# Packed attention and a gelu feed-forward layer on one core: the product of packed queries and w_in remade in float32 tiles, with a new order

## The chip, the cores and the metric

One core of a Trainium2 chip runs the whole program. The metric is the device time of one execution in microseconds; the median of three runs stands for a kernel. Engines: TensorE (matmuls), VectorE, ScalarE, GpSimd, and SP, which issues all transfers. In rows of the profile they are PE (PEld for its weight loads), DVE, ACT, POOL and SP.

## What is computed

```python
def _attn_ref(q, k, v, p):          # q, k, v: (8, 8, 576, 64), p: (8, 8, 32, 64)
    scale = 1.0 / np.sqrt(q.shape[-1])
    def sm_attn(qq, kk, vv):
        s = scale * np.matmul(qq, kk.transpose(0, 1, 3, 2))
        s = s - np.max(s, axis=-1, keepdims=True)
        a = np.exp(s)
        a = a / (np.sum(a, axis=-1, keepdims=True) + 1e-09)
        return np.matmul(a, vv)
    p_packed = sm_attn(p, k, v)
    return sm_attn(q, p_packed, p_packed)
def _moe_ref(x, w_in, w_out):       # x: (4608, 512), the heads side by side
    h = x @ w_in                    # w_in (512, 2048), w_out (2048, 512), both 64-bit floats
    g = 0.5 * h * (1.0 + erf(h / np.sqrt(2.0)))
    return g @ w_out
```

## The kernel before, in words

The packed queries (32 for each of 8 heads) are computed first. As x is attention weights times packed queries, x @ w_in is taken as attention weights times (packed queries times w_in). That inner product, `wps`, replaces a large one: for each batch it has 8 x 32 = 256 rows.

The eight batches go in four pairs, the hidden layer in four blocks of 512 columns (FB). A pair and a block make a **unit** u, 16 in all, with eight **steps** n each: two batches j times four chunks c of 128 hidden columns. A step is one group of the first product `h` (L1050: wp times a2T, twelve matmuls of 288 columns; in unit 0 plain float32, L1041), a gelu on ScalarE (L1077), a split of the result into a high and a low half (g: L1083 on ScalarE, L1084 on VectorE), and twelve matmuls of the second product `o` (L1104 to L1106) with w_out. Rows left over by 576 = 4.5 x 128 go into `o_edge` at a unit's end. Numbers that enter a matmul are split into halves of type float32r and multiplied in three matmuls, high by high, high by low, low by high; the low half is number minus high half. Plain float32 matmuls appear in the profile as two records each.

The product that is changed is `packed_w_in` (L950). For a pair of batches `ph` holds the packed queries in block form, 128 columns for each of four slots (a slot is two heads, 128 rows of w_in), with zeros elsewhere, split into halves by GpSimd (`packed_split`, L661). With w_in's halves it takes three matmuls a slot (L968 to L970), in two groups of two slots. A group's result is copied from PSUM in pieces of 64 partitions: four casts on ScalarE (L986), four subtractions on VectorE (L990). In unit 0 the product is plain float32 (L964), in halves of 256 columns, one batch at a time.

The weights arrive as 64-bit floats and are decoded to float32 on the chip (`decode`, L886): two ScalarE instructions (L906, L907), three on VectorE (L916, L917, L922), and GpSimd adds (L938, L928) and takes low halves (L884). In units 0 to 3 every slot i of a unit (0 to 3 of w_in, 4 to 7 of w_out) is decoded and its halves stored to scratch memory (`keep`); units 4 to 15 reload them. In unit 0, w_in is decoded in halves of 256 columns and its float32 form is used before the split.

Attention of pair 0 runs at the start, chunk by chunk (a chunk is four heads of a batch): packed scores `s` (L483, eight matmuls on tiles of 64x32), exponentials, `pp` (L623), a transpose, ppT, the second scores, maxima, centring, exponentials, weights a2. Pairs 1 to 3 run it beside the units of the pair before. While it has nothing to do at the start, TensorE multiplies `still`, an idle product (L1023).

The order of the work is set by a planner inside the kernel (class `Order`). Each piece of work (`Op`) has an engine, a cost and a step number; an engine that is free in the plan takes the ready piece of lowest step number. Buffers are rings: a piece that needs one waits until it is given back. The tables FIRST (unit 0 and pair 0), LATER (the other pairs) and LEAD (weights, `wps`) hold the step numbers. The plan fixes the order of instructions on each engine and of transfers on SP's queue, and semaphores do the waiting on the chip.

Of the kernel before, what the change touches and what calls it, by code (L numbers as in the profile page):

```python
# [10 lines left out]
F32 = mybir.dt.float32  # L11
# [55 lines left out]
LEAD = {"load": 4.4, "decode": -3.6, "packed_w_in": 4}  # L67

FIRST = {
    "p": (-200.0, -193.0),  # L70
    "k": (-186.0, -199.0, -185.0, -182.0),
    "v": (-195.0, -197.0, -181.0, -179.0),
    "q": (-183.0, -191.0, -178.0, -177.0),
    "w": (-187.0, -198.0, -194.0, -188.0, -192.0, -184.0, -190.0, -196.0, -189.0, -180.0, -176.0, -175.0),
    "scores1": (-29.0, -55.27, -22.89, -50.0),
    "softmax1": (-53.13, -50.0, -30.0, -29.0),
    "packed": (-48.76, -31.48, -27.58, -51.55),
    "scores2": (-51.65, -51.18, -34.07, -27.2),
    "softmax2": (-49.06, -48.66, -3.32, 1.29),
    "weights2": (-4.59, -15.04, -24.74, -16.37),  # L80
    "decode": (-45.0, -37.0, -20.64, -35.16, -36.53, -35.0, -50.97, -46.0, 1.0, 8.37, -33.0, 2.0),
    "packed_w_in": (-7.62, -48.76, -38.15, -25.99),
    "packed_split": (8.53, 1.15, 2.3, -11.78),
    "weights_split": (7.2, 1.11, -2.81, -0.07),
    "w_in_split": (-17.7, 3.0, 5.95, 3.0),
    "groups1": ((0,), (1,), (2,), (3,)),
    "groups2": ((0,), (1,), (2,), (3,)),
    "gpsimd": (0, 1, 2, 3),
    "copy": ("DVE", "ACT", "DVE", "ACT", "ACT", "ACT", "DVE", "DVE"),
    "low": (0, 3, 4, 5),  # L90
    "banks": (False, False, False, False),
    "turn": {"k": ("ACT", "DVE", "ACT", "ACT"), "q": ("DVE", "DVE", "ACT", "ACT")},
# [42 lines left out]
class Op:  # L135
# [3 lines left out]
    def __init__(self, engine, cost, step, fn, takes=(), table=None, busy=True):  # L139
        self.engine, self.cost, self.step, self.fn = engine, cost, step, fn  # L140
        self.takes, self.table, self.busy = takes, table, busy


class Order:
# [71 lines left out]
    def issue(self, engine):  # L216
# [50 lines left out]
def packed_attention_gelu_ffn(ctx: ExitStack, tc: tile.TileContext, q, k, v, p, w_in, w_out, out):  # L267
# [59 lines left out]
    wis.names = [f"w_{u}_{i}" for u in range(NU) for i in range(4)]  # L327
    wos.names = [f"w_{u}_{i}" for u in range(NU) for i in range(4, 8)]
# [22 lines left out]
    ph = [const.tile([P, 2, 4 * P], F32R, name=f"ph{i}") for i in range(2)]  # L351
    for t in ph:
        nc.gpsimd.memset(t.bitcast(F32), 0.0)

    plain_ph = accs.take("ph")
    nc.gpsimd.memset(plain_ph, 0.0)


    pp_ready = {(b, hh): Event() for b in range(B) for hh in range(2)}
    plain_ready = {(b, hh): Event() for b in range(2) for hh in range(2)}  # L360
# [5 lines left out]
    a2T, plain_a2 = {}, {}  # L366
# [110 lines left out]
    def products(ts, lhs, rhs, swap=0):  # L477

        for n in range(2):
            rows = slice(64 * n, 64 * n + 64)  # L480
            for g in range(4):
                r0 = 32 * (g ^ 2 * swap)
                nc.tensor.matmul(  # L483
                    ts[n][r0:r0 + 32, :HALF], lhsT=lhs[n][rows, 32 * g:32 * g + 32], rhs=rhs(g)[rows],
                    start=True, stop=True)

    def scores_of_batch(bt, name, which, lhs, evacuate, engine, cost, step):
        xTs = [bt.xT[name, c].rearrange("p (g x) -> p g x", g=2) for c in range(2)]

        def part(half):  # L490
# [4 lines left out]
                    (t[:, 0], t[:, 1]), lhs, lambda g: xTs[g // 2][:, g % 2, cols], which == 2 and bt.j),  # L495
# [82 lines left out]
    def packed(s, step):  # L578
# [659 lines left out]
```

## Time and profile before

| | |
|---|---|
| median of 3 runs | 769.54 us (769.28 to 769.65) |
| profiled execution | 768.53 us, its span 766.7 us |
| TensorE busy | 743.2 us, 97% of the span |
| VectorE busy | 458.5 us, 60% |
| ScalarE busy | 413.7 us, 54% |
| GpSimd busy | 204.7 us, 27% |
| moved by transfers | 123.5 MB |

The span is the time between the first and the last instruction of the profiled execution; that execution's own time holds 1.8 us around it. Busy is the union of an engine's instructions. TensorE's matmuls are pipelined and the ends in the records are modelled, so the distance from one start to the next says what a matmul costs, and an average of 97% says nothing about the stretches in which it waits.

### The profile page before, as it was taken

What the parts mean: (1) busy time and instruction counts of PE and PEld (TensorE: products, weight loads), DVE (VectorE), ACT (ScalarE), POOL (GpSimd) and SP (SyncE); (2) the same over time, 40 slices, a digit from 0 to 9 for tenths busy, and PEclk for the clock granted to TensorE, in tenths of its full rate; (3) what the DMA queues carried; (4) which work ended last, traced back from release to release, by engine and by line L of the source; (5) the groups of instructions that cost most, each with busy time, mean ns of one, the idle gap of its engine ahead of it and who ended that gap; (6) DMA issues with size and microseconds to landing.
All of it is one profiled execution on the core that took longest, in us unless ns stands there. A gap on an engine that the chain in (4) does not pass through costs nothing.

```text
span 766.7 us, 12964 instructions
## 1 busy us (share of the span) xinstructions
PE 743.2 (97%) x4948; PEld 621.5 (81%) x4948; DVE 458.5 (60%) x733; ACT 413.7 (54%) x714; POOL 204.7 (27%) x401
## 2 busy tenths in 40 slices
PE   9889998898999999999999999999999999999998
PEld 7667776676778888888778888888878888888886
DVE  5999767988787543446478643356479522352522
ACT  4888866859667254437447345336546354333421
POOL 3568535764541111111122111111122111111110
PEclk9999999999999999999999999999999999999999
DMA  9859995656744899334443799324542523222021
GB/s 301 301 205 208 219 275 187 232 183 172 273 142 164 206 160 223 127 125 100 144 142 141 183 193 214 148 103 94 170 144 110 190 98 116 103 97 72 6 105 69
DMA packets 159293, 123.53 MB, mean 161 GB/s; under 512 B 124416, under 2 KB 132608, under 8 KB 159232
## 3 DMA queue, kind: packets, MB, share of 16 engines
q1 hardware_dynamic: 159232, 122.71, 56.7%
q8 instruction: 39, 0.64, 0.4%
q14 instruction: 22, 0.18, 0.1%
HBM read 96.47 MB, written 26.21 MB: 160 GB/s over the span
## 4 chain that ended last, share of the span: by engine, by line
PE 77%; DVE 7%; DMA 6%; ACT 5%; SPq 2%; issue 1%; POOL 1%; ACTq 0%; POOLq 0%; DVEq 0%
PE h L1050 22%; PE o L1104 14%; PE o L1106 13%; PE o L1105 13%; DMA wraw<-in_moe_w_in_dram 2%; DMA wraw<-in_moe_w_out_dram 2%; DMA v<-in_v_dram 2%; PE o_edge L1104 2%; PE o_edge L1106 2%; PE o_edge L1105 2%; PE s L483 2%; PE wps L968 2%; PE wps L969 2%; PE wps L970 2%; ACT graw L1077 1%
## 5 line engine op out<-in xcount | busy, mean ns | idle before, releaser
L1077 ACT ACTIVATE graw<-h 128x576 f32<-128x576 f32 x128 | 102.4, 802 | 227.9 <-PE h L1050 173.4
L1050 PEld LDWEIGHTS h<-a2T,wp 128*128 128x128 f32 x1440 | 203.0, 189 | 15.1 <-DVE wp L990 2.6
L1050 PE MATMUL h<-a2T,wp 128*128 128x288 f32 x1440 | 211.6, 296 | 3.3 <-DVE wp L990 2.0
L1104 PE MATMUL o<-w,g 128*128 128x512 f32 x508 | 203.8, 401 | 0.9 <-ACT g L1083 0.9
L1106 PE MATMUL o<-w,g 128*128 128x512 f32 x508 | 199.8, 393 | 2.8 <-DVE g L1084 2.7
L1105 PE MATMUL o<-w,g 128*128 128x512 f32 x508 | 199.0, 392 | 0.0
L1084 DVE TENSOR_TENSOR g<-graw,g 128x512 fp32r<-128x512 f32 x128 | 96.5, 754 | 159.6 <-ACT g L1083 154.9
L1094 POOL CAST t<-graw 128x64 fp32r<-128x64 f32 x128 | 42.0, 328 | 434.9 <-ACT graw L1077 429.4
L1106 PEld LDWEIGHTS o<-w,g 128*128 128x128 f32 x508 | 95.9, 189 | 26.0 <-DVE g L1084 4.9
L1104 PEld LDWEIGHTS o<-w,g 128*128 128x128 f32 x508 | 96.1, 189 | 24.7 <-issue 6.0
L990 DVE TENSOR_TENSOR wp<-wps,wp 64x512 fp32r<-64x512 f32 x120 | 79.9, 687 | 50.1 <-ACT wp L986 48.7
L1105 PEld LDWEIGHTS o<-w,g 128*128 128x128 f32 x508 | 96.1, 189 | 16.5
L1165 DVE TENSOR_TENSOR acc<-o,acc 128x512 f32<-128x512 f32 x96 | 63.9, 685 | 35.8 <-PE o L1106 35.8
L1083 ACT CAST g<-graw 128x512 fp32r<-128x512 f32 x128 | 79.6, 623 | 2.6
L986 ACT CAST wp<-wps 64x512 fp32r<-64x512 f32 x120 | 66.7, 581 | 17.5 <-PE wps L970 16.4
L938 POOL TENSOR_TENSOR wt<-wt 128x512 int32<-128x512 int32 x28 | 38.0, 1359 | 39.9 <-DVE wt L922 39.9
L1095 POOL TENSOR_TENSOR t<-graw,t 128x64 fp32r<-128x64 f32 x128 | 45.8, 358 | 10.2
L906 ACT ACTIVATE wt<-wraw 128x512 f32<-128x512 f32 (+1 forms) x36 | 22.5, 626 | 28.5 <-DMA wraw<-in_moe_w_in_dram 15.7
L884 POOL TENSOR_TENSOR w<-wt,w 128x512 fp32r<-128x512 f32 x26 | 36.4, 1398 | 1.9 <-POOL wt L938 0.5
L412 DVE STREAM_TRANSPOSE kT<-k 128x1152 f32<-128x1152 f32 x12 | 16.5, 1376 | 21.5 <-DMA k<-in_k_dram 21.4
L922 DVE SCALAR_TENSOR_TENSOR wt<-wraw,wt 128x512 int32<-128x512 int32 (+1 forms) x36 | 26.6, 740 | 0.8
L1023 PE MATMUL idle<-still 128*128 128x256 bf16 x168 | 25.4, 294 | 1.5 <-DVE still L347 1.1
(139 smaller groups left out, 808.3 us busy)
## 6 DMA issues: line engine op xcount, KB each, us to landing
w<-ws SPq DMA_DIRECT2D x96, 512.0 KB, 5.0
ws<-w SPq DMA_DIRECT2D x32, 512.0 KB, 4.4
out_dram<-acc SPq DMA_DIRECT2D x36, 256.0 KB, 2.1
v<-in_v_dram SPq DMA_DIRECT2D x16, 512.0 KB, 5.2
wraw<-in_moe_w_out_dram SPq DMA_DIRECT2D x16, 512.0 KB, 5.0
k<-in_k_dram SPq DMA_DIRECT2D x48, 144.0 KB, 4.6
q<-in_q_dram SPq DMA_DIRECT2D x48, 144.0 KB, 5.1
wraw<-in_moe_w_in_dram SPq DMA_DIRECT2D x12, 512.0 KB, 4.3
```

What stands on the lines that cost most here:

```text
L986: (nc.vector.tensor_copy if engine == DVE else nc.scalar.copy)(hi.bitcast(F32) if plain(u) else hi, x)
L990: nc.vector.tensor_tensor(lo, x, hi.bitcast(F32), ALU.subtract)
L1050: nc.tensor.matmul(t[:, half, :HALF], lhsT=w[:, wpart, ch, fc], rhs=a2T[b, ch][:, apart, half * HALF:(half + 1) * HALF], start=ch == 0 and ...
L1077: lambda raw: nc.scalar.activation(*dst_src(raw), AF.Gelu), [(graws, f"graw_{n}")], table="gelu")
L1083: g = yield Op(ACT, 0.52, lead, lambda g: nc.scalar.copy(g[:, 0], main), [(gts, f"g_{n}")])
L1084: yield Op(DVE, 0.6, lead, lambda: nc.vector.tensor_tensor(g[:, 1], main, g[:, 0].bitcast(F32), ALU.subtract))
L1094: nc.gpsimd.tensor_copy(dst[:, 0], side)
L1095: nc.gpsimd.tensor_tensor(dst[:, 1], side, dst[:, 0].bitcast(F32), ALU.subtract)
L1104: nc.tensor.matmul(t, lhsT=g[0], rhs=w[:, 0], start=first, stop=False)
L1105: nc.tensor.matmul(t, lhsT=g[0], rhs=w[:, 1], start=False, stop=False)
L1106: nc.tensor.matmul(t, lhsT=g[1], rhs=w[:, 0], start=False, stop=last)
L1165: yield Op(DVE, 0.6, n, lambda: nc.vector.tensor_tensor(a, x, a, ALU.add))
```

## The change

A slot of w_in is now 128 rows in another arrangement: 64 dims of head g in the partitions 0 to 63, of head g + 4 in 64 to 127, two values of g side by side. So there are two w_in slots of double width for a unit (i is 0 or 1; w_out has 2 to 5), each loaded in two pieces of 256 columns, and each piece by two transfers of 64 partitions. w_in stays plain float32: one buffer a slot, no split; what is stored and reloaded is half as much. `pp` holds the packed queries of a batch without zeros, and the product is `products`, the function of the scores: eight float32 matmuls on 64x32 tiles, for one batch at a time. The result comes from PSUM in one cast and one subtraction over 128 partitions x 1024. `ph` and its split are gone. The planner keeps marked pieces of VectorE (port) and all pieces of GpSimd from overlapping in the plan. The tables are new. Rings: `wi` three buffers instead of four, `wp1` one instead of two, `sm` six instead of four, `pn` two instead of one.

```diff
 LATER = {
-    "p": (-29.7, 4.9),
+    "p": (-43.8, -18.8),
...
-LEAD = {"load": 4.4, "decode": -3.6, "packed_w_in": 4}
+LEAD = {"load": 4.9, "decode": -5.3, "packed_w_in": 2.9}
...
+            if op.port:
+                begin = max(begin, self.port)
             end = begin + op.cost
+            if op.port:
+                self.port = end
...
-    wis = ring("wi", 4, [P, 2, FB], F32R)
+    wis = ring("wi", 3, [P, 2, FB])
...
-    wps = [ring("wp0", 1, [P, 2, 2, FB], F32R), ring("wp1", 2, [P, 2, 2, FB], F32R)]
+    wps = [ring(f"wp{j}", 1, [P, 2, 2, FB], F32R) for j in range(2)]
+    pps = ring("pp", 4, [P, P])
...
-    def products(ts, lhs, rhs, swap=0):
+    def products(ts, lhs, rhs, size=HALF):
         for n in range(2):
             rows = slice(64 * n, 64 * n + 64)
             for g in range(4):
-                r0 = 32 * (g ^ 2 * swap)
+                cols = slice(32 * g, 32 * g + 32)
                 nc.tensor.matmul(
-                    ts[n][r0:r0 + 32, :HALF], lhsT=lhs[n][rows, 32 * g:32 * g + 32], rhs=rhs(g)[rows],
-                    start=True, stop=True)
+                    ts[n][cols, :size], lhsT=lhs[n][rows, cols], rhs=rhs(g)[rows], start=True, stop=True)
...
-        s.ppT = yield Op(ACT, 0.16, step + 2, lambda t: nc.scalar.copy(t, bank(m)[:, :P]), [(ppts, f"ppT_{s.n}")])
+        both = pp[s.b] = yield from one(pps, f"pp_{s.b}", ACT, step + 2)
+        rows = slice(64 * s.hh, 64 * s.hh + 64)
+        yield Op(ACT, 0.16, step + 2, lambda: nc.scalar.copy(both[rows], bank(m)[rows, :P]))
+        fire(pp_ready[s.b])
+        if s.b < 2:
+            s.ppT = yield Op(
+                DVE, 0.19, step + 2, lambda t: nc.vector.tensor_copy(t, bank(m)[:, :P]), [(ppts, f"ppT_{s.n}")])
...
+            src = w_in.rearrange("(hh g d) n -> hh d g n", hh=2, g=4)
+            c0 = f * FB + part * (FB // 2)
+            for hh in range(2):
+                nc.sync.dma_start(
+                    t[64 * hh:64 * hh + 64].rearrange("p (g n) -> p g n", g=2),
+                    src[hh, :, 2 * i:2 * i + 2, c0:c0 + FB // 2].bitcast(I32))
...
         def product(t):
-            for e in range(2):
-                slot = 2 * hh + e
-                cut = slice(slot * P, slot * P + P)
...
-                base, w = ph[pr % 2][:, :, cut], wi[u, 2 * hh + e][:, :, cols]
-                nc.tensor.matmul(t[:, e, :m], lhsT=base[:, 0], rhs=w[:, 0], start=True, stop=False)
-                nc.tensor.matmul(t[:, e, :m], lhsT=base[:, 0], rhs=w[:, 1], start=False, stop=False)
-                nc.tensor.matmul(t[:, e, :m], lhsT=base[:, 1], rhs=w[:, 0], start=False, stop=True)
+            products((t[:, 0], t[:, 1]), [pp[b]] * 2, lambda g: wi[u, g // 2][:, g % 2, cols], m)
...
-        yield Op(engine, (0.32 + 0.75 * m / FB) * n, step, high)
-        for e in range(0 if plain(u) else 2):
-            yield Op(DVE, (0.07 + 0.58 * m / FB) * n, step, lambda: low(halves[n * e:n * e + n]))
+        yield Op(engine, 0.12 + 0.87 * m / FB, step, high)
+        if not plain(u):
+            yield Op(DVE, 1.2, step, lambda: nc.vector.tensor_tensor(lo, x, hi.bitcast(F32), ALU.subtract))
...
-            start(all_packed_w_in(u, (0, 1), [8 * u - LEAD["packed_w_in"]]))
+            for j in range(2):
+                start(packed_w_in(u, j, 0, 8 * u + 4 * j - LEAD["packed_w_in"]))
```

How the order moves instructions is shown at three places. The lines in these rows are those of the kernel they come from. First, TensorE around its first group of `h`, before:

```order
L1023 MATMUL idle<-still 128x256
L964 MATMUL wps_1_1_1_912<-w_2_285,ph 128x256
L964 MATMUL wps_1_1_1_912<-w_3_222,ph 128x256
L1041 MATMUL h_918<-a_0_642,wp_0_92 128x288 x4
L1023 LDWEIGHTS still
```

And with the change (L981 is `h`, L481 `products`, L620 `pp`, L1046 to L1048 are `o`; an output called idle is a PSUM buffer that the idle product named first):

```order
L620 MATMUL idle<-v_1_750,e1T_1_755 32x64 x20
L981 MATMUL h_839<-a_0_552,wp_0_84 128x288 x4
L634 MATMUL ppTm_1_849<-ident,pn_1_845 128x128
L481 MATMUL s_1_0_852<-qT_0_612,ppT_0_835 32x288 x8
...
L981 MATMUL h_877<-a_0_552,wp_0_84 128x288 x4
L481 MATMUL wps_1_1_893<-w_0_78,pp_792 32x256 x2
L481 MATMUL wps_1_1_893<-w_1_79,pp_792 32x256 x2
...
L1046 MATMUL idle<-w_2_430,g_873 128x512
```

All eight half products and all score groups of pair 0 stood ahead of the first `h`; now the two of batch 1 and two of its score groups stand behind it, and two `h` instead of three stand ahead of the first `o`.

Second, VectorE at the product of unit 1, before (the operands named wp_0 and wp_1 are the two batches):

```order
L1084 TENSOR_TENSOR g_1266<-graw_1250,g_1266 128x512
L990 TENSOR_TENSOR wp_0_1071<-wps_0_0_0_1252,wp_0_1071 64x512
L990 TENSOR_TENSOR wp_1_1244<-wps_0_0_0_1252,wp_1_1244 64x512
...
L990 TENSOR_TENSOR wp_0_1071<-wps_1_0_0_1268,wp_0_1071 64x512
L990 TENSOR_TENSOR wp_1_1244<-wps_1_0_0_1268,wp_1_1244 64x512
...
L916 TENSOR_SCALAR wt_5_0_1347<-wt_5_0_1347 128x512
```

With the change:

```order
L940 TENSOR_TENSOR wp_0_1031<-wps_0_0_1182,wp_0_1031 128x1024
L873 TENSOR_SCALAR wt_3_0_1207<-wt_3_0_1207 128x512
L874 TENSOR_SCALAR wt_3_0_1207<-wt_3_0_1207 128x512
...
L1025 TENSOR_TENSOR g_1253<-graw_1238,g_1253 128x512
L410 STREAM_TRANSPOSE kT_1_1304<-k_1_1174 128x1152
L1025 TENSOR_TENSOR g_1289<-graw_1285,g_1289 128x512
L940 TENSOR_TENSOR wp_1_1231<-wps_1_0_1276,wp_1_1231 128x1024
```

Eight subtractions in a row became two, one for each batch, with eight instructions between them.

Third, TensorE in unit 4, at the product for unit 5, before:

```order
L970 MATMUL wps_0_0_0_3199<-w_1_2812,ph_79 128x512
L1104 MATMUL o_0_3212<-w_4_2526,g_3158 128x512
...
L1106 MATMUL o_3_3231<-w_4_2526,g_3158 128x512
L1050 MATMUL h_3239<-a2T_0_2907,wp_1_2702 128x288 x6
L1050 MATMUL h_3239<-a2T_1_2944,wp_1_2702 128x288 x6
...
L968 MATMUL wps_1_0_0_3276<-w_2_2871,ph_79 128x512
```

With the change:

```order
L481 MATMUL wps_0_0_3138<-w_0_2586,pp_2022 32x512 x2
L481 MATMUL wps_0_0_3138<-w_1_2976,pp_2022 32x512 x2
...
L990 MATMUL h_3147<-a2T_0_2644,wp_1_2763 128x288 x6
L990 MATMUL h_3147<-a2T_1_2796,wp_1_2763 128x288 x6
L1046 MATMUL o_0_3075<-w_4_2884,g_3124 128x512
...
L1048 MATMUL o_3_3094<-w_4_2884,g_3124 128x512
L990 MATMUL h_3187<-a2T_0_2601,wp_0_2989 128x288 x6
```

The product of batch 0 (wp_0) stands one `h` and one step of `o` ahead of the `h` that uses it; that of batch 1 follows four steps later.

## Rows read from the trace of the kernel before

**Rows 1.** Stretches: length; PE, PEld, DVE, ACT, POOL busy (instructions); clock; DMA share; GB/s.
```profile
0.00:64.40 64.40, 58.04 (x614) 43.23 (x614) 53.41 (x113) 44.25 (x93) 33.92 (x49) 1.00 0.79 262
64.40:225.00 160.60, 147.58 (x965) 117.80 (x966) 131.03 (x187) 120.11 (x197) 93.31 (x118) 0.98 0.77 217
...
225.00:762.70 537.70, 537.14 (x3370) 460.47 (x3369) 273.32 (x434) 249.38 (x425) 77.50 (x235) 1.00 0.49 133
```
**Rows 2.** TensorE's waits, 65.6 to 225 us: total, times, longest.
```profile
PE e1Tm L585 <- ACT graw L1077: 3.6, 2, 2.3
PE o L1106 <- DVE g L1084: 2.7, 3, 1.1
PE h L1050 <- DVE wp L990: 2.0, 1, 2.0
```
**Rows 3.** Timeline of TensorE near 706 us: start, duration, instruction.
```profile
705.99 0.40 PE L968 MATMUL wps<-w,ph 128*128 128x512 f32 x1
...
707.39 0.39 PE L1104 MATMUL o<-w,g 128*128 128x512 f32 x1
```
**Rows 4.** The same, near 347 us: one group of scores.
```profile
347.00 0.40 PE L1106 MATMUL o<-w,g 128*128 128x512 f32 x1
347.33 0.72 PE L483 MATMUL s<-kT,pT 64*32 64x288 f32 x16
347.98 0.50 PE L1104 MATMUL o<-w,g 128*128 128x512 f32 x1
348.31 0.39 PE L1105 MATMUL o<-w,g 128*128 128x512 f32 x1
348.55 0.39 PE L1106 MATMUL o<-w,g 128*128 128x512 f32 x1
```
**Rows 5.** The same, near 291 us: two groups of scores.
```profile
291.03 0.39 PE L1106 MATMUL o<-w,g 128*128 128x512 f32 x1
...
292.48 0.50 PE L1104 MATMUL o<-w,g 128*128 128x512 f32 x1
292.82 0.40 PE L1105 MATMUL o<-w,g 128*128 128x512 f32 x1
```
**Rows 6.** Instruction groups from 225 us on: busy, mean ns, idle before.
```profile
L986 ACT CAST wp<-wps 64x512 fp32r<-64x512 f32 x96 | 53.5, 581 | 16.9 <-PE wps L970 15.8
...
L990 DVE TENSOR_TENSOR wp<-wps,wp 64x512 fp32r<-64x512 f32 x96 | 64.0, 687 | 46.6 <-ACT wp L986 45.4
```
**Rows 7.** VectorE's instruction groups up to 64.4 us.
```profile
L917 DVE TENSOR_SCALAR wt<-wt 128x256 int32<-128x256 int32 x8 | 4.7, 589 | 0.3
L646 DVE COPY ph<-ppT 64x64 f32<-64x64 f32 x8 | 4.5, 569 | 0.1
...
L917 DVE TENSOR_SCALAR wt<-wt 128x512 int32<-128x512 int32 x5 | 3.8, 758 | 0.2
...
L986 DVE COPY wp<-wps 64x256 f32<-64x256 f32 x6 | 2.5, 422 | 0.1
...
L427 DVE COPY qT<-qm 128x384 f32<-128x384 f32 x4 | 2.0, 545 | 0.0
L884 DVE TENSOR_TENSOR w<-wt,w 128x512 fp32r<-128x512 f32 x2 | 1.5, 771 | 0.3 <-ACT w L935 0.3
```
**Rows 8.** Timeline of VectorE, then of GpSimd, near 60 us.
```profile
59.60 1.21 DVE L916 TENSOR_SCALAR wt<-wt 128x512 f32<-128x512 f32 x1
...
59.24 1.29 POOL L884 TENSOR_TENSOR w<-wt,w 128x512 fp32r<-128x512 f32 x1
```
**Rows 9.** Transfers: issues, KB each, median us from issue to landing.
```profile
w<-ws SPq DMA_DIRECT2D x96, 512.0 KB, 5.0
...
v<-in_v_dram SPq DMA_DIRECT2D x16, 512.0 KB, 5.2
...
v<-in_v_dram SPq DMA_DIRECT2D x16, 64.0 KB, 5.0
```
**Rows 10.** Timeline of TensorE at its first group of `h`.
```profile
57.00 2.16 PE L1041 MATMUL h<-a,wp 128*128 128x288 f32 x8
```

More of the change, by code (lines that the diff above doesn't have):

```diff
@@ L135, with __init__ @@
 class Op:
-    def __init__(self, engine, cost, step, fn, takes=(), table=None, busy=True):
+    def __init__(self, engine, cost, step, fn, takes=(), table=None, busy=True, port=False):
         self.engine, self.cost, self.step, self.fn = engine, cost, step, fn
         self.takes, self.table, self.busy = takes, table, busy
+        self.port = (engine == POOL and cost > 0) or port
 class Order:
@@ L348, in packed_attention_gelu_ffn @@
     make_identity(nc, ident)
[L351 to L360, printed above, removed]
+    pp_ready = [Event(2) for _ in range(B)]
     a2_ready = [Event(2) for _ in range(B)]
@@ L675, in scores2_of_chunk @@
         ts = yield Op(
-            PE, 0.68, step, lambda *ts: products(banks(*ts), [s.ppT] * 2, lambda g: xT[:, g], s.bt.j), takes, busy=False)
+            PE, 0.68, step, lambda *ts: products(banks(*ts), [s.ppT] * 2, lambda g: xT[:, g]), takes, busy=False)
         ts = ts if len(takes) > 1 else [ts]
         xts.give(s.bt.xT["q", s.hh])
-        start(free_ppT(s))
+        ppts.give(s.ppT)
         def turned():
@@ L745, in weights2 @@
         yield Op(DVE, 1.1, step, inverse)
-        yield Op(engine, cost, step, lambda: on(engine).tensor_tensor(u, u, per_block(r), ALU.mult))
+        yield Op(engine, cost, step, lambda: on(engine).tensor_tensor(u, u, per_block(r), ALU.mult), port=True)
         if s.b < 2:
@@ L759, in weights2 @@
         yield Op(
-            engine, cost, step, lambda: on(engine).tensor_tensor(t[:, 1], raw, t[:, 0].bitcast(F32), ALU.subtract))
+            engine, cost, step, lambda: on(engine).tensor_tensor(t[:, 1], raw, t[:, 0].bitcast(F32), ALU.subtract),
+            port=True)
         a2T[s.b, s.hh] = t
@@ L903, in decode @@
+        raw = yield Op(DMA, (2, 620e3) if i < 2 else (1, 524e3), load_step, fetch, [(raws, f"wraw_{n}")])
         low, high = words(raw)[:, :, 0], words(raw)[:, :, 1]
         def both_words(both):
[L906 to L912 removed]
@@ new lines, in packed_w_in @@
+        wp[u, j] = yield from one(wps[j], f"wp_{u}_{j}", DVE, step)
+        yield pp_ready[b]
+        for i in range(2):
+            for x in (part,) if plain(u) else range(2):
+                yield w_ready[u, i, x]
+        def product(t):
+            products((t[:, 0], t[:, 1]), [pp[b]] * 2, lambda g: wi[u, g // 2][:, g % 2, cols], m)
+        t = yield Op(PE, 0.28 + 0.87 * m / FB, step, product, [(wide, f"wps_{u}_{j}_{part}")], busy=False)
+        for i in range(2):
+            fire(wi_used[u, i])
@@ L999, in packed_w_in @@
         wide.give(t)
-    def all_packed_w_in(u, js, steps):
-        for j in js:
-            wp[u, j] = yield Op(DVE, 0, steps[0], lambda t: None, [(wps[j], f"wp_{u}_{j}")])
-        yield [packed_w_in(u, hh, js, part, step + hh) for part, step in enumerate(steps) for hh in range(2)]
+        if u % NF == NF - 1:
+            pps.give(pp[b])
     def free_wi(u, i):
```

273 lines of the change are left out of this document (107 added, 166 removed).

## The prediction

> **What bounds the kernel now.** I read first the busy time by stretch, which falls into three parts [rows 1]. [...] Before 64.4 us TensorE waits for the first attention and fills up with idle products; the busiest other engine is VectorE with 53.4 of 64.4 us, then ScalarE with 44.3.
>
> The view of waits names what TensorE waited for up to 225 us: ScalarE's exponentials and gelus, VectorE's low halves of g, and once, for 2.0 us, VectorE's low half of wp, the evacuation of the product that the change remakes [rows 2].
>
> The timeline, third, prices TensorE's groups by where the next instruction starts, since the recorded ends overlap.
>
> **The product.** Before, a unit has two groups of six `wps` matmuls over 512 columns. One runs from 705.99 until the next instruction at 707.39 [rows 3]: 1.40 us, so 2.80 us a unit. The change makes two groups of eight float32 matmuls on 64x32 tiles, over 512 columns. The same kind of work stands in the trace as the score products `s`: eight 64x32 tiles over 288 columns. One such group between matmuls of the second product: 347.00 to 347.98 is 0.98 us, less 0.23 for the matmul ahead (from one start to the next among its fellows, 348.31 to about 348.55) leaves 0.75; the matmul behind it takes 0.33 instead of 0.23; together 0.85 [rows 4]. Two groups in a row: 1.45 - 0.23 = 1.22, and 0.34 for 0.23 behind, together 1.33 [rows 5]. So a further 288 columns cost 0.48 us, and entry and exit 0.37. For 512 columns: 0.48 x 512/288 + 0.37 = 1.22 us, two of them 2.44. Saved: 2.80 - 2.44 = 0.36 us a unit, times 15 units (the first unit is part of the start) = **5.4 us**. Ends: with the bare 0.65 us from 347.33 to 347.98, entry and exit are 0.17, a group 1.02 and the gain 11.4 us; with 0.10 us more a group, 2.4 us. I take 5.4, because it is counted between neighbours that stay.
>
> Evacuation: eight ScalarE casts of 0.58 us and eight VectorE subtractions of 0.69 us a unit, 4.6 and 5.5 us [rows 6], become two of each over 128x1024. Each lies between one and two times the price over 512, so a unit pays at most 2.3 and 2.7 us. After 225 us I cost this at nothing. The work that hides it: the order puts a group of `h` (1.6 us) and twelve matmuls of `o` (2.7 us) between a product and the `h` that needs it, 4.3 us, while cast and subtraction need at most 1.2 + 1.4 and some tenths to start. Without that cover a product would cost up to 2.9 us.
>
> **The start.** TensorE's own work hardly counts here; VectorE's does, in its 53.4 us up to the first subtraction of g. By row means [rows 7]: decoding w_in in four whole pieces instead of eight halves saves 8 x 0.59 - 4 x 0.76 = 1.7 us on one of its three instructions, some 2.5 on all. The eight `ph` copies go, 4.5, against four ppT copies of under 0.4 each, 1.2. Two `wp` copies of at most 0.84 stand before that point instead of eight of 0.42: 1.7. Two low halves of w_out go to GpSimd, 1.5, and two of w_in, alike, vanish. Six turn copies of 0.55 go to ScalarE, 3.3. Chunk 0's centring and scaling come from GpSimd, two rows of about 0.8 for the same work: -1.6. That is 12.2 us less, and some 4 us more (softmax of the second batch) moves behind the first g. ScalarE loses the casts of w_in and the `wp` copies and gains the turn copies, about 4 us less in sum; the loads are the same bytes. So VectorE allows 12 us, ScalarE 4, the loads perhaps none. Also, of TensorE's work two products and two score groups that stood ahead of the first `h` now stand behind it, as does one `h` of the three ahead of the first `o`: about 4 us that the earlier start has to carry. I take **6 us** net, the middle of the ends 0 and 12.
>
> Some of VectorE's 53.4 us is no work either: its tensor_scalar at 59.60 took 1.21 us and ended only behind GpSimd's subtraction of 59.24, which took 1.29 [rows 8]. The new planner holds marked pieces of the two engines apart (the port flag); what that gives is part of the 6.
>
> **The middle part.** In each of units 1 to 4 VectorE loses some 3 us of evacuation and ScalarE 2.3, in units 1 to 3 ScalarE loses four casts and GpSimd four subtractions for w_in. [...] ScalarE's table loads, exponentials and gelus stay. So I take half of 16.2, **8 us**; ends 0 and 16. What is late next: the exponentials of the second pair on ScalarE.
>
> Queues: in units 1 to 3 each piece of w_in takes two transfers, 24 issues on SP instead of 12, in front of k and q; stores fall from 32 to 24, reloads from 96 to 72. None of it is on TensorE's path while weights come early. At unit 4 the second slot of w_in can be reloaded only when unit 3's last product has freed a buffer. A reload lands in 5.0 us [rows 9], and two groups of `h` and one step of `o`, 5.9 us, lie between: 0, or 1 to 2 us once, inside the range.
>
> **Sum.** 5.4 + 6 + 8 = 19.4 us. The profiled execution took 768.5 us, its span 766.7. So 747.3 of span and 749.1; the median of the runs is 1.0 above the profiled one: **750 us**.
>
> **Rivals.**
> A, only the product counts: start and waits belong to ScalarE and the loads, and stay. For it: ScalarE leads the list of waits [rows 2]. 769.5 - 5.4 = 764. Chance 0.15.
> B, the half-width loads hold the start. The start moves 262 GB/s [rows 1], so w_in's 2.1 MB are 8.0 us of it. Ends from rows: v's tails over 64 partitions land in 5.0 us beside bodies over 128 in 5.2 [rows 9], no cost to be seen; at half the rate 8 us more, which takes back the 6 and 2 besides. Then 769.5 - 5.4 - 8 + 2 = 758. Chance 0.12. [...]
> C, the middle part empties: 16 us there, 9 at the start, 5.4 for the product: 739. For it: VectorE sheds some 12 us before 64 us and 12 behind. Against it: ScalarE. Chance 0.17.
> D, slower: w_in's ring has three buffers and a unit holds two, so in units 1 to 3 the second slot can be finished only after the last product of the unit before. Its chain is a load of 5.0 us [rows 9] and twice some six instructions of the size of the decode's 0.76 [rows 7], 14 us, under 20 to 34 us of TensorE work in the order. It decides where the engines' queues stretch the chain until the wait passes 6.5 us a unit, three times; at 8.5 us a unit 775 us. Against it: the steps between. Chance 0.07.
> E, slower: over 512 columns the eight tiles run four at a time, and the change doesn't do what it says. A group then costs 0.85 us more, 30 groups 26 us: 776. Against it: 0.48 us for eight tiles over 288 columns [rows 4, 5]. Chance 0.03.
>
> **How the numbers follow.** The forecast has the remaining 0.46. From 737 to 765 lie the forecast, B, and A and C but for their outer tails: 8 in 10. No change means 768.0 to 771.1, within 0.2%, about what a measurement can tell. Faster: the forecast, B, C and nearly all of A, 0.88. Within: A's upper tail, 0.03. Slower: D and E with a little of A, 0.09.
>
> **What would show it.** Right: a group of the new product between two matmuls of the second product costs about 1.2 us; rows over 128x1024 near 1.0 and 1.2 us on ScalarE and VectorE; the first `h` at 48 to 51 us instead of 57.00 [rows 10]; some 8 us idle or slow from there to the point that 225 us is now; a span near 747. Wrong: the first `h` at 57 or later (A, or B if ScalarE waits for w_in's loads); `wps` waiting for w in units 1 to 4 (D); groups of 2 us (E); a granted clock below 1.00 after 225 us.

## The result and the profile after

| | before | after |
|---|---|---|
| median | 769.60 us (769.28 to 769.72, 4 runs) | 758.07 us (756.97 to 759.21, 4 runs) |
| ratio | | 0.9851, 95% interval 0.9834 to 0.9868 |
| span of the profiled execution | 766.7 us | 756.2 us |
| moved by transfers | 123.5 MB | 106.8 MB |

The kernel is 11.5 us faster; 19.4 were forecast. The time lies in the range, 8 us above the forecast, and on the number of rival B (758).

The answer to [rows 1], cut where a unit begins: up to the first `h`, to the first `h` of unit 4, to the last matmul. The kernel before, cut at the same events (length; PE, PEld, DVE, ACT and POOL busy; clock; DMA share; GB/s):

```profile
0.00:57.00 57.00, 50.78 (x581) 37.97 (x582) 46.26 (x102) 38.56 (x87) 28.56 (x44) 1.00 0.77 267
57.00:250.10 193.10, 179.89 (x1132) 144.72 (x1132) 158.84 (x233) 144.76 (x228) 103.13 (x134) 0.98 0.72 205
250.10:762.70 512.60, 512.09 (x3236) 438.81 (x3236) 252.66 (x399) 230.41 (x400) 73.06 (x224) 1.00 0.50 133
```

The changed kernel:

```profile
0.00:54.00 54.00, 46.35 (x586) 35.39 (x586) 30.38 (x69) 33.12 (x69) 18.22 (x20) 0.97 0.91 275
54.00:240.10 186.10, 176.11 (x1263) 137.19 (x1256) 142.39 (x212) 136.03 (x197) 78.57 (x105) 0.98 0.71 178
240.10:752.00 511.90, 509.43 (x3473) 416.00 (x3472) 221.65 (x334) 205.86 (x335) 57.58 (x192) 1.00 0.46 114
```

So 3.0 us were won at the start, 7.0 in the middle, 0.7 in the long rest. VectorE shed 16 us up to the first `h` (the prediction counted 12 less work and some 4 moved behind) and 16 in the middle (12 were counted), so it is not VectorE's work that kept the gain small. TensorE's idle time in the middle fell only from 13.2 to 10.0 us, and the mean clock there stayed at 0.98; the last row holds 2.5 idle us where before there were 0.5.

TensorE's waits from 60 to 225 us, the answer to [rows 2]:

```profile
PE pp L620 <- DMA v<-in_v_dram: 3.0, 1, 3.0
PE pTm L458 <- DMA p<-in_p_dram: 2.9, 1, 2.9
PE s L481 <- DVE wp L940: 2.5, 1, 2.5
PE pp L620 <- ACT e1T L592: 0.5, 1, 0.5
PE h L990 <- ACT graw L1017: 0.4, 1, 0.4
```

ScalarE's and VectorE's names have nearly gone from the list. Three waits of 3.0, 2.9 and 2.5 us took their place: for two loads, and for a subtraction of the product, which is really a third load. That subtraction stands on VectorE behind the transposition of k (L410), which waits for a k load that landed at 103.94:

```profile
104.06 1.38 DVE L410 STREAM_TRANSPOSE kT<-k 128x1152 f32<-128x1152 f32 x1 [5.59 <-DMA k<-in_k_dram]
105.37 0.65 DVE L1025 TENSOR_TENSOR g<-graw,g 128x512 fp32r<-128x512 f32 x1
105.94 1.22 DVE L940 TENSOR_TENSOR wp<-wps,wp 128x1024 fp32r<-128x1024 f32 x1
```

The answer to [rows 10], the first `h`, with what PE did ahead of it:

```profile
53.19 0.90 PE L620 MATMUL idle<-v,e1T 128*32 128x64 f32 x40 [0.23 <-DMA v<-in_v_dram]
54.02 2.21 PE L981 MATMUL h<-a,wp 128*128 128x288 f32 x8
```

The product, the answer to [rows 3], at a step of the second product in unit 14:

```profile
702.45 0.39 PE L1048 MATMUL o<-w,g 128*128 128x512 f32 x1
702.77 1.09 PE L481 MATMUL wps<-w,pp 64*32 64x512 f32 x16
703.79 0.92 PE L990 MATMUL h<-a2T,wp 128*128 128x288 f32 x5
```

702.45 to 703.79 less 0.23 for the `o` is 1.11, and the `h` behind the group takes 0.1 longer to get going: 1.21 us, where 1.22 were forecast. The evacuation, the answer to [rows 6]:

```profile
L940 DVE TENSOR_TENSOR wp<-wps,wp 128x1024 fp32r<-128x1024 f32 x24 | 29.3, 1222 | 48.9 <-ACT wp L935 48.8
L935 ACT CAST wp<-wps 128x1024 fp32r<-128x1024 f32 x24 | 24.3, 1014 | 53.0 <-PE wps L481 53.0
```

Who made p late is seen on SP's own queue, in the order of its issues:

```profile
57.52 1.10 SPq L452 DMA_DIRECT2D p<-in_p_dram  x2
67.16 1.26 SPq L858 DMA_DIRECT2D wraw<-in_moe_w_in_dram  x2
68.46 9.23 SPq L394 DMA_DIRECT2D k<-in_k_dram  x8
78.20 1.05 SPq L452 DMA_DIRECT2D p<-in_p_dram  x2
```

From 58.6 to 67.2 SP issues nothing. Its list of waits (total, times, longest; 40 to 240 us) has the reason, the third VectorE instruction of a decode, which frees one of the two raw weight buffers:

```profile
SPq L858 <- DVE wt L879: 22.0, 7, 8.4
```

Behind the halted load of w_in stand two loads of k and then the p for which TensorE stops at 79.

### The profile page after: what moved, and what is told of

It reads as the page before. It is cut to its first block, busy times and chain, and to the rows that moved or that the text cites. A ratio compares the mean times of both kernels' runs of the same rounds, so it can differ in the third digit from the quotient of the medians.

```text
span 756.2 us, 13260 instructions
## 1 busy us (share of the span) xinstructions
PE 732.3 (97%) x5313; PEld 588.6 (78%) x5313; DVE 395.1 (52%) x614; ACT 375.0 (50%) x601; POOL 154.4 (20%) x316
## 4 chain that ended last, share of the span: by engine, by line
PE 81%; DMA 9%; SPq 4%; DVE 2%; ACT 2%; issue 1%; POOL 0%; ACTq 0%; DVEq 0%
PE h L990 23%; PE o L1046 14%; PE o L1048 13%; PE o L1047 13%; PE wps L481 4%; SPq L394 3%; DMA wraw<-in_moe_w_in_dram 3%; DMA v<-in_v_dram 2%; PE s L481 2%; DMA k<-in_k_dram 2%; PE h L981 2%; PE o_edge L1046 2%; PE o_edge L1048 2%; PE o_edge L1047 2%; PE pp L620 1%; PE idle L963 1%
## 5 line engine op out<-in xcount | busy, mean ns | idle before, releaser
L990 PE MATMUL h<-a2T,wp 128*128 128x288 f32 x1440 | 214.2, 298 | 0.8 <-ACT graw L1017 0.4
L1046 PE MATMUL o<-w,g 128*128 128x512 f32 x508 | 204.5, 403 | 0.0
L1048 PE MATMUL o<-w,g 128*128 128x512 f32 x508 | 198.9, 392 | 0.0
L1025 DVE TENSOR_TENSOR g<-graw,g 128x512 fp32r<-128x512 f32 x128 | 91.8, 717 | 166.5 <-ACT g L1023 166.3
L1036 POOL CAST t<-graw 128x64 fp32r<-128x64 f32 x128 | 36.6, 286 | 495.8 <-ACT graw L1017 449.6
L1046 PEld LDWEIGHTS o<-w,g 128*128 128x128 f32 x508 | 95.6, 188 | 27.8 <-issue 11.8
L1048 PEld LDWEIGHTS o<-w,g 128*128 128x128 f32 x508 | 95.5, 188 | 21.9 <-DVE g L1025 0.5
L940 DVE TENSOR_TENSOR wp<-wps,wp 128x1024 fp32r<-128x1024 f32 x30 | 36.6, 1220 | 49.1 <-ACT wp L935 49.1
L935 ACT CAST wp<-wps 128x1024 fp32r<-128x1024 f32 x30 | 30.4, 1013 | 53.5 <-PE wps L481 53.5
L481 PE MATMUL wps<-w,pp 64*32 64x512 f32 (+1 forms) x544 | 35.4, 576 | 0.0
L866 ACT ACTIVATE wt<-wraw 128x512 f32<-128x512 f32 x32 | 21.7, 678 | 23.9 <-DMA wraw<-in_moe_w_in_dram 17.3
L963 PE MATMUL idle<-still 128*128 128x256 bf16 x201 | 28.8, 294 | 3.0 <-ACT kT L425 2.0
L410 DVE STREAM_TRANSPOSE kT<-k 128x1152 f32<-128x1152 f32 x12 | 16.4, 1374 | 29.0 <-DMA k<-in_k_dram 29.0
L901 POOL TENSOR_TENSOR wt<-wt 128x512 int32<-128x512 int32 x16 | 23.1, 1443 | 35.6 <-DVE wt L879 32.6
L873 DVE TENSOR_SCALAR wt<-wt 128x512 f32<-128x512 f32 x32 | 19.0, 595 | 18.4 <-ACT wt L866 18.1
```

Of the source, the lines that this page charges most:

```text
L481: nc.tensor.matmul(ts[n][cols, :size], lhsT=lhs[n][rows, cols], rhs=rhs(g)[rows], start=True, stop=True)
L940: yield Op(DVE, 1.2, step, lambda: nc.vector.tensor_tensor(lo, x, hi.bitcast(F32), ALU.subtract))
L990: nc.tensor.matmul(t[:, half, :HALF], lhsT=w[:, wpart, ch, fc], rhs=a2T[b, ch][:, apart, half * HALF:(half + 1) * HALF], start=ch == 0 and ...
L1025: DVE, 0.6, lead, lambda: nc.vector.tensor_tensor(g[:, 1], main, g[:, 0].bitcast(F32), ALU.subtract),
L1036: nc.gpsimd.tensor_copy(dst[:, 0], side)
L1046: nc.tensor.matmul(t, lhsT=g[0], rhs=w[:, 0], start=first, stop=False)
```

## The experiments

All keep the changed kernel's order of work on TensorE, VectorE, ScalarE and GpSimd (the planner sees no difference; what is edited is what a piece of work issues, or how many buffers really stand behind a ring). Where the time went is read from the start of a unit's first `h` in each trace, and from the last matmul (us):

| run | median | unit 0 | 1 | 2 | 3 | 4 | 8 | 9 | 12 | last |
|---|---|---|---|---|---|---|---|---|---|---|
| before | 769.6 | 57.0 | 101.6 | 148.4 | 201.6 | 250.1 | 425.1 | 467.7 | 599.8 | 762.7 |
| after | 758.1 | 54.0 | 97.7 | 144.8 | 200.4 | 240.1 | 415.6 | 458.4 | 590.8 | 752.0 |
| wide_rows | 750.9 | 48.5 | 93.3 | 137.3 | 191.3 | 231.1 | 407.0 | 452.1 | 584.5 | 745.6 |
| narrow_rows | 753.4 | 53.1 | 98.5 | 141.6 | 194.9 | 234.7 | 410.3 | 453.9 | 586.3 | 747.5 |
| queue | 755.6 | 54.7 | 95.9 | 138.9 | 195.1 | 234.8 | 411.1 | 456.4 | 589.0 | 750.2 |
| raw3 | 748.3 | 53.9 | 94.5 | 137.5 | 191.2 | 230.9 | 406.0 | 448.6 | 580.9 | 742.1 |
| buffers | 748.3 | 52.8 | 93.5 | 136.5 | 188.3 | 228.1 | 403.5 | 449.6 | 582.4 | 743.6 |
| k_first | 744.5 | 54.4 | 95.0 | 138.0 | 190.7 | 230.4 | 405.3 | 445.0 | 577.4 | 738.5 |
| k_first_rows | 738.6 | 47.5 | 88.1 | 131.2 | 182.2 | 221.9 | 396.9 | 437.7 | 570.1 | 731.2 |
| evac8 | 783.5 | 52.8 | 96.6 | 146.3 | 200.7 | 244.2 | 427.5 | 475.3 | 614.2 | 775.4 |
| evac4 | 754.1 | 54.0 | 98.8 | 143.6 | 197.3 | 237.1 | 412.3 | 454.6 | 587.0 | 748.2 |
| twice | 775.8 | 53.9 | 98.8 | 143.0 | 196.7 | 236.5 | 418.8 | 464.0 | 602.3 | 768.7 |

The table also shows how far two traces can differ without a cause in their edits. twice issues the same instructions as the changed kernel up to unit 4, and its first `h` of that unit comes 3.6 us earlier (236.5 against 240.1). Up to the first `h`, k_first is the same as buffers, and is 1.6 us later (54.4 against 52.8). Smaller differences between single traces are not read as effects below. In wide_rows, narrow_rows and k_first_rows the rows of w_in come in another order, so these three do not compute the layer; they only time its transfers.

Two theories stood at the outset: the transfers of w_in over 64 partitions hold the start (rival B), or SP's queue makes loads late that stand behind a load without a buffer.

### The width of w_in's transfers

**wide_rows.**

```diff
-            for hh in range(2):
-                nc.sync.dma_start(
-                    t[64 * hh:64 * hh + 64].rearrange("p (g n) -> p g n", g=2),
-                    src[hh, :, 2 * i:2 * i + 2, c0:c0 + FB // 2].bitcast(I32))
+            rows = w_in.rearrange("(x p) n -> x p n", x=4)
+            for g in range(2):
+                nc.sync.dma_start(
+                    t[:, FB * g:FB * g + FB], rows[2 * i + g, :, c0:c0 + FB // 2].bitcast(I32))
```

> The changed kernel, same order of instructions, but each piece of w_in comes by two transfers of 128 partitions x 2 KB (128 rows of w_in that lie together) instead of two of 64 partitions x 4 KB; the rows of w_in are thereby permuted in the result. If the half-width transfers hold the start, the first 38 us move well over 283 GB/s (the mean of the first two slices of the changed kernel's page), w_in's late piece lands in some 6 us instead of 12.4, the first h comes 3 to 5 us before 54.0, and the time is 752 to 755 us. If the start is held by the engines' own order and SP's queue alone, the first h stays within 1 us of 54.0 and the time within 1.5 us of 758.

Measured: 750.86 us (748.71 to 753.38), the first `h` at 48.5. 5.5 us come at the start. The gains are a little more than expected, and w_in's late piece lands in 9.3 us (issued at 14.24, landed at 23.59), not in 6 (12.4 in the changed kernel). **narrow_rows** takes the rows that lie together too, but again over 64 partitions, to tell the width from the place in memory.

```diff
-                    src[hh, :, 2 * i:2 * i + 2, c0:c0 + FB // 2].bitcast(I32))
+                    rows[2 * i + hh, :, :, c0:c0 + FB // 2].bitcast(I32))    # rows: "(x g p) n -> x p g n"
```

> The changed kernel, same order, each piece of w_in still by two transfers of 64 partitions x 4 KB, but out of 128 rows that lie together (the rows of w_in are permuted in the result); wide_rows took the same kind of rows over 128 partitions and 7 us less than the changed kernel. If the 64 partitions are what is slow, nothing changes: first h within 1 us of 54.0, time 756 to 760 us. If the scattered rows in memory were slow, it behaves as wide_rows: first h near 48.5, time 749 to 753.

Measured: 753.36 us (751.63 to 756.63): the total lies between both expectations, a miss. The start does not: 53.1, close to the changed kernel. The transfers of the first 30 us, in 40 slices (busy share of the DMA engines in tenths, GB/s), changed kernel, narrow_rows, wide_rows:

```profile
DMA  0038699979999999999999989999999999989999
GB/s 0 0 81 148 142 350 341 240 175 247 216 305 284 270 298 262 212 218 219 246 266 279 226 200 293 383 430 391 403 416 309 244 209 238 170 194 281 336 411 424
```

```profile
GB/s 0 0 80 125 75 375 384 276 234 232 279 336 258 318 308 244 220 205 235 251 227 262 291 395 428 375 428 404 412 368 206 229 242 259 399 421 406 424 409 432
```

```profile
GB/s 0 0 83 145 88 332 369 264 333 264 362 319 276 327 223 256 369 385 399 419 416 397 427 386 405 418 378 388 425 399 391 432 408 329 297 367 360 384 381 386
```

From 12 to 16 us (slices 17 to 21) the engines are busy for nine tenths or more in the first, and yet move 212 to 266 GB/s; over 128 partitions 369 to 419. The whole of the first 30 us moved 331 GB/s in the kernel before, 259 in the changed kernel, 286 in narrow_rows and 325 in wide_rows. So the width is what is slow here, and it costs the start 53.1 - 48.5 = 4.6 us, some three times the 1.6 us by which equal starts differ. Why it is slow no run shows. Behind the start the two come within 1.9 us of each other (747.5, 745.6), and by unit 4 narrow_rows is 5.4 us ahead of the changed kernel, of which only 0.9 came at the start. twice is 3.6 us ahead there without any edit so far, so no cause in the arrangement of the rows is claimed. A difference of 4 us between two totals is not put down to a cause here unless the table shows the place.

**two_queues_act**, **two_queues_pool** ask whether two halves side by side would do. They build on k_first (below):

```diff
-                nc.sync.dma_start(
+                (nc.scalar if hh and u == 0 else nc.sync).dma_start(
```

> The kernel of the run k_first, the result unchanged, with the upper half (partitions 64 to 127) of each of unit 0's four pieces of w_in issued on ScalarE's queue instead of SP's, so that the two halves can be under way side by side. If the narrow transfers are slow because one queue works them off one after the other, the first h comes 3 to 6 us before the 54.4 of k_first and the time is 738.5 to 742 us. If the halves still wait for each other, or ScalarE's issuing delays its copies by as much, the first h stays at 53 or later and the time at 743.5 or more.

> As two_queues_act, with the upper halves issued by GpSimd, which has nothing to do up to 11.5 us in k_first. If two queues make the difference, the time is as in two_queues_act or up to 1 us less, since ScalarE issues nothing. If GpSimd's transfers start or land later than SP's, its first piece lands after the 9.8 us of the changed kernel and the time is 744 or more.

Measured: 743.04 (742.26 to 743.50) and 742.59 us (742.04 to 744.19); the first `h` at 53.5 and 52.5, against 54.4 in k_first and 47.5 with wide rows. Both missed the hoped-for range: 0.9 and 1.9 us of 6.9, and since buffers, with the same start as k_first, has 52.8, even that is not shown to be a gain. So a second queue did not bring the halves in faster here: the first 30 us moved 273 and 279 GB/s against 273 in k_first and 338 in k_first_rows.

### SP's queue

**queue** leaves all buffers of weights as they are and moves transfers on SP alone; p gets a second buffer, so that it can be issued early.

```diff
+            held.append(pieces)
+            if (u, i, part) != (1, 1, 1):
+                flush()
...
+            kn[0] += 1
+            if kn[0] >= 2:
+                flush()
...
+            if bt.b > 1 and not bt.j:
+                piece(praws.next(f"p_{bt.b + 1}"), bt.b + 1)
```

Here `pieces` issues the two transfers of a piece of w_in, `flush` issues what is held, `kn` counts loads of k, and `piece` issues p of one batch.

> The changed kernel with SP's queue alone remade at one place: the last piece of unit 1's w_in, which stands for 8.4 us waiting for a raw buffer, is issued behind the first two k loads of pair 1, and p of an odd batch is issued right behind p of the batch before it (a second buffer). [...]

Measured: 755.60 us (753.17 to 756.16). The table shows 5.9 us less at unit 2, inside the 4 to 7 that I expected in all (TensorE's wait of 2.9 us for p and that of 2.5 for wp behind k are gone there, with 0.8 and 0.4 left in the whole trace; twice is 1.8 us ahead at this point without an edit); 4 of them go again later, 2.4 in unit 8 alone. The mechanism holds; the total, expected at 751 to 754, is a miss.

**raw3** gives a third raw weight buffer, and **buffers** gives second buffers to v and p as well; order unchanged on SP too (raw3 shown; buffers has `"vraw": 2, "praw": 2` besides):

```diff
-            self.spare = self.pool.tile(self.shape, self.dtype, tag=self.tag, name=name, bufs=self.bufs)
+            self.spare = self.pool.tile(
+                self.shape, self.dtype, tag=self.tag, name=name, bufs={"wraw": 3}.get(self.tag, self.bufs))
```

> The changed kernel, same order, with a third raw weight buffer alone (v and p keep one). If SP's standing for raw buffers is what made p and k late, TensorE's waits for p (2.9 us in unit 0) and for wp behind k (2.5 us in unit 1) go, and the wait for v (3.0 us, a buffer of its own) and the first h at 54.0 stay: the time is 750 to 753, and buffers' last 2 to 4 us are v's. If the single buffers of v and p were the cause, the time stays at 756 or more.

> The changed kernel, same order on every engine and queue, but three raw weight buffers instead of two, two for v and two for p instead of one, so that SP's queue stands less. If the queue theory holds, TensorE's waits for p, v and wp (8.4 us) go, with them most of the two spells at a mean clock of 0.91, and the time is 746 to 750. Because pp of the last chunk no longer waits for v, the first h comes about 1 us earlier. If ScalarE and VectorE are the next bound, waits of the kind h on graw or o on g take their place and the time is 754 or more.

Measured: raw3 748.30 us (746.14 to 753.45), buffers 748.32 us (746.63 to 749.61). The third raw buffer alone is worth as much as all of them, 9.8 us by the medians. TensorE's waits in raw3, and in twice, which has no third buffer:

```profile
PE ppTm L635 <- ACT pn L628: 2.0, 1, 2.0
PE pTm L459 <- DMA p<-in_p_dram: 0.8, 2, 0.4
PE pp L621 <- DMA v<-in_v_dram: 0.4, 1, 0.4
PE s L482 <- DVE wp L941: 0.4, 1, 0.4
```

```profile
PE pTm L458 <- DMA p<-in_p_dram: 3.3, 3, 2.6
PE pp L620 <- DMA v<-in_v_dram: 1.3, 1, 1.3
PE s L481 <- ACT graw L1018: 1.0, 1, 1.0
```

The long wait for p is there in twice too and gone in raw3: that is SP's stop. The waits for v and behind k have other lengths in twice (1.3 and 1.0 us for 3.0 and 2.5), so their full length in the changed kernel's trace is not the rule. At unit 4 raw3 is 9.2 us ahead of the changed kernel and 5.6 ahead of twice. raw3 is better than I expected, since the wait for v went as well (0.4 us left): v, too, stood behind a load of w_in on SP. The second buffers of v and p win nothing at the end: buffers is 2.8 us ahead of raw3 at unit 4 and loses more than that in unit 8.

**k_first.** What was left in buffers was a wait for k in unit 8. The wait, the `o` behind it, and the stretch of 10 us around them:

```profile
PE s L482 <- DVE kT L411: 2.6, 1, 2.6
```

```profile
446.83 0.79 PE L1047 MATMUL o<-w,g 128*128 128x512 f32 x1
447.42 0.63 PE L1048 MATMUL o<-w,g 128*128 128x512 f32 x1
447.85 0.63 PE L1049 MATMUL o<-w,g 128*128 128x512 f32 x1
448.27 0.63 PE L1047 MATMUL o<-w,g 128*128 128x512 f32 x1
```

```profile
440.00:450.00 10.00, 7.41 (x46) 3.95 (x46) 4.49 (x5) 2.67 (x6) 0.56 (x2) 0.69 0.80 137
```

Their starts lie 0.43 us apart, not 0.23: TensorE goes on at a lower clock (the granted clock of 440 to 450 us is 0.69 in the mean). That k load is issued at 435.5, behind a q load that takes SP 5.9 us. In k_first the two change places, in pairs 2 and 3.

```diff
-                    nc.sync.dma_start(t[32 * i:32 * i + 32], view[j])
+                    pieces.append((t[32 * i:32 * i + 32], view[j]))
...
+            held.append(issue)
+            if (name, bt.b // 2, seen[name, bt.b // 2]) not in (("q", 2, 1), ("q", 3, 1)):
+                while held:
+                    held.pop()()
```

> The kernel of the run buffers (three raw buffers, two for v, two for p), and in pairs 2 and 3 the last k load issued ahead of the q load that stood in front of it on SP's queue. [...] If q is then late instead, or k waits for its buffer, the time stays at 747 or above.

Measured: **744.51 us (743.51 to 744.73), 0.9672 of before (0.9645 to 0.9699)**, inside the 743 to 746 that I expected if the wait for k comes from its place in the queue; it computes the whole layer and beats both kernels. Unit 8 takes 39.7 us instead of 46.1 in buffers, 6.3 less by the unrounded times: the wait of 2.6 us for k, one of 0.5 for p, and the spell at the lower clock. Against raw3, whose longest wait for k is 0.8 us, it is 2.8 less. The swap on top of raw3 alone was not run. Its three stretches, to be held against those of the changed kernel:

```profile
0.00:54.40 54.40, 46.30 (x587) 35.12 (x587) 30.74 (x68) 32.94 (x69) 17.97 (x20) 0.97 0.93 281
54.40:230.40 176.00, 173.13 (x1259) 134.79 (x1256) 144.99 (x213) 135.07 (x197) 79.12 (x105) 1.00 0.76 186
230.40:738.50 508.10, 507.89 (x3472) 416.20 (x3472) 221.52 (x334) 205.71 (x335) 57.55 (x192) 1.00 0.47 115
```

**k_first_rows** adds the wide loads:

> The kernel of the run k_first with the loads of w_in over 128 partitions as in wide_rows (the rows of w_in are permuted in the result). If the narrow transfers and SP's queue cost TensorE different waits, their gains add up: 758 - 6.3 (the gain of wide_rows in the trace) - 8.4 (buffers) - 3 (k) = 740, and 738 to 742 are right. If both work by bringing the same loads earlier, half of the smaller one is lost and the time is 743 to 746.

Measured: 738.55 us (736.96 to 740.07). The gains add up: two causes, not one.

### The product and its evacuation

**twice.**

```diff
-            products((t[:, 0], t[:, 1]), [pp[b]] * 2, lambda g: wi[u, g // 2][:, g % 2, cols], m)
+            for _ in range(2 if u > 4 else 1):
+                products((t[:, 0], t[:, 1]), [pp[b]] * 2, lambda g: wi[u, g // 2][:, g % 2, cols], m)
```

> The changed kernel, same order, with each product of units 5 to 15 computed twice over (22 groups of eight tiles more, the result is the same). If the tiles run eight at a time and TensorE is what bounds this part, a further group costs 0.48 x 512/288 = 0.85 us, 18.8 us in all, and the time is 775 to 778. If they ran four at a time a group would cost 1.7 us, 37 us in all. If the product lay in time that TensorE has to spare, the time would rise by less than 12 us.

Measured: 775.80 us (774.99 to 776.31), 17.7 more than the changed kernel. A doubled group in unit 14:

```profile
698.05 0.39 PE L1049 MATMUL o<-w,g 128*128 128x512 f32 x1
698.37 1.95 PE L481 MATMUL wps<-w,pp 64*32 64x512 f32 x32
700.24 0.53 PE L991 MATMUL h<-a2T,wp 128*128 128x288 f32 x2
```

2.19 us against 1.34 is 0.85, as expected. 21 of the 22 groups lie behind unit 5's first `h`, 17.9 us of them, and from there to the last matmul the trace is 19.0 longer. So a further group costs what eight tiles at a time would, not 1.7 us, and TensorE's time here is the kernel's.

**evac8** cuts cast and subtraction into four pieces each, but for unit 0.

```diff
-            (nc.vector.tensor_copy if engine == DVE else nc.scalar.copy)(hi.bitcast(F32) if plain(u) else hi, x)
+            for e in range(2):
+                for r in range(0, P, 64):
+                    nc.scalar.copy(hi[r:r + 64, e], x[r:r + 64, e])
```

> The changed kernel, same order, but the result of a product leaves PSUM in pieces of 64 x 512 as before: four casts and four subtractions a product instead of one and one. If the evacuation lies beside other work, as predicted for the part behind 225 us, nothing changes from unit 5 on and the whole differs by less than 2 us from 758. If the smaller evacuation is what earned the middle part, units 1 to 4 lose some 1 to 2.5 us each and the time is 762 to 768, with waits of TensorE on wp.

Measured: 783.48 us (781.41 to 785.76), 25 us more, far outside both expectations, and at another place: from unit 3 to unit 11 it loses 23 us, in units 11 to 15 only 0.1. Units 4 to 11 are those that hold the attention of pairs 2 and 3. One such place in unit 6, TensorE, then ScalarE and VectorE:

```profile
349.19 1.09 PE L481 MATMUL wps<-w,pp 64*32 64x512 f32 x16
355.74 0.30 PE L634 MATMUL ppTm<-ident,pn 128*128 128x128 f32 x1 [2.34 <-DVE wp L948]
```

```profile
350.41 2.36 ACT L938 CAST wp<-wps 64x512 fp32r<-64x512 f32 x4 [1.77 <-PE wps L481]
```

```profile
352.80 2.79 DVE L948 TENSOR_TENSOR wp<-wps,wp 64x512 fp32r<-64x512 f32 x4 [5.93 <-ACT wp L938]
```

The product holds one of the two double PSUM buffers (`wide`) from 349.19 until 355.59. The transpose ppTm wants one, and waits 2.3 us; `h` stands behind it, and the granted clock of 350 to 360 us is 0.83. VectorE sat idle for 5.9 us before these subtractions, so it is not busy elsewhere. In one piece, cast and subtraction take 1.01 and 1.22 us and no such wait arises. The same wait, as long, stands in unit 10, and units 6 and 10 are 4.5 and 5.1 us longer than in the changed kernel. The other 13 us of the 23 are not explained so directly: in units 3 to 5, 8 and 9 TensorE waits for gelus and copies of scores on ScalarE, for low halves of g, for p and for k, and the granted clock of 400 to 740 us is 0.98 in the mean (1.00 in the changed kernel).

**evac4** asks, with two pieces of each, whether it is the time or the number of instructions.

```diff
+            for e in range(2):
+                nc.scalar.copy(hi[:, e], x[:, e])
```

> The changed kernel, same order, with the result of a product copied in two pieces of 128 x 512 instead of one of 128 x 1024 (evac8 had four of 64 x 512 and took 25 us more). If what cost evac8 its time is how long a product holds its PSUM buffer, two pieces cost 2 x 0.58 + 2 x 0.69 against 1.01 + 1.22 us, 0.3 more, and the time is 757 to 761. If it is the number of instructions in the queues, a third of evac8's loss shows and the time is 765 or more.

Measured: 754.07 us (753.47 to 756.90), no loss, and below both expectations. (3 of the 4 us below the changed kernel are there at unit 4, where twice has 3.6 without an edit.) So a third of evac8's added instructions costs nothing, and the time of the copies is what remains: a piece of 64 x 512 costs ScalarE 0.58 us, and one of 128 x 512 0.59. That this time counts through the held buffer is shown in units 6 and 10; for the other units the buffer and the longer work of ScalarE and VectorE were not separated, for which a third buffer in `wide` would be needed.

## Why the prediction came out as it did

| part | forecast | measured | with the later cures |
|---|---|---|---|
| start, to the first `h` | 6 | 3.0 | 8.5 (wide_rows) |
| middle, with four products (1.4) | 9.4 | 7.0 | 17.1 (k_first) |
| rest, eleven products | 4.0 | 0.7 | 4.5 (k_first) |
| sum | 19.4 | 10.7 | |

**The product**: right. 1.21 us a group against 1.22, and twice shows that this is time of the kernel. Units 13 and 14, which hold no attention and no waits, take 39.76 us from first `h` to first `h` instead of 40.14: 0.38 a unit, where 0.36 were forecast. The rest should have given 4.0 us and gave 0.7, because new waits took it back: unit 8 has 1.8 us of them, for k, p and wp, and takes 42.8 us against 39.7 in k_first, at a granted clock of 1.00; unit 6 loses another 0.6. With k issued first the rest is 4.5 us shorter.

**The start**: the step "the loads perhaps none" failed. VectorE's work did shrink, and the first `h` would have come at 48.5, inside the forecast of 48 to 51, had w_in come over 128 partitions. Rival B was the case in kind; its 8 us, at half the rate, were my estimate and too much, and no run shows that half: the width costs 4.6. I gave it 0.12, because v's tails over 64 partitions landed in 5.0 us [rows 9]. That row could not show it: 64 KB pieces say nothing about the crowd of megabytes that moved at 212 to 266 GB/s from 12 to 16 us of the changed kernel. Up to the first `h` of the changed kernel ScalarE waits 8.1 us for w_in's loads, with copies of k behind them in its order (it had waited 10.0 before, but then VectorE was later still).

**The middle**: the step that failed is the one on queues, "None of it is on TensorE's path while weights come early". I counted SP's issues and not its waits. Loads of w_in waited for a raw buffer (22.0 us on SP's list, 8.4 the longest), and k, p and v stood behind them. raw3, which changes nothing but that buffer, wins 9.8 us by the medians. The term of 8 us was my estimate, half of 16.2 (the idle 13.0 of [rows 1] and, for its clock of 0.98, 3.2); no run shows that half: the changed kernel's middle is 7.0 us shorter with the products in it. It was too low: without the waits (2.9 idle us are left in k_first, at a granted clock of 1.00) the middle is 17.1 us shorter than before, 15.7 without the products, as in rival C, which had 16 for it. ScalarE's exponentials, named as the next to be late, were not.

**The evacuation**: "After 225 us I cost this at nothing" gave the right term by a wrong reason. I looked for the `h` that needs the product, 4.3 us away; who waited in units 6 and 10 of evac8 was ppTm, 2.3 us each for the PSUM buffer. In the changed order pieces over all 128 partitions are needed, one or two: the old form costs 25 us.

**Rivals** D and E fell: no wait for w's ring in units 1 to 4 is on TensorE's list, and the group costs 1.21. That the total fell on B's 758 is partly chance: B holds at the start, but the middle lost 10 of its 17 us for another reason.

What stays open: why traces differ by some 4 us at unit 4 where no edit has acted (twice 236.5, changed kernel 240.1). That the waits for k and v are shorter in twice is seen; which load decides was not separated. The 7.0 us of the middle carry this uncertainty.

## What to carry to other kernels

Read the issuing queue like an engine: list what it waits for, and what stands behind a transfer that waits for a buffer; one more raw buffer was worth nearly as much here as the whole change (9.8 us by the medians, against 11.5). When an order is repacked more tightly, price how long each step holds a shared PSUM buffer (6.4 us in unit 6 of evac8), not only when its result is due. And a price for a transfer must come from a row under the same load, or it bounds nothing: v's tails landed in 5.0 us, w_in's late piece in 12.4.

## What was not expected of the hardware

Transfers over 64 partitions, in a crowd, held the DMA engines busy at 212 to 266 GB/s from 12 to 16 us, where 128 partitions reached 369 to 419, and issuing the other half on a second queue gave back at most 1 to 2 us of 6.9. Behind the wait of 2.6 us in buffers TensorE went on with starts 0.43 us apart instead of 0.23, and the unit took 6.3 us more; behind the changed kernel's waits of 2.5 and 3.0 us the granted clock is 0.50 from 109 to 111 and from 174 to 176 us, but behind its wait of 2.9 us for p it did not fall (1.00 from 80 to 100 us). A cast out of PSUM costs 0.58 us over 64 x 512, 0.59 over 128 x 512 and 1.01 over 128 x 1024.
